# Attention's side work cut into halves: products with wo and 13 of 48 score units over two pairs of steps each, and the steps of the division set further apart

## The chip, the cores and the metric

The kernel runs on one core of a Trainium2 chip. The metric is the device time of one execution in microseconds (us). The kernel before takes 1585.26 us (median of 3 runs, 1582.82 to 1586.16).

## The reference

A transformer block on 2048 tokens of 448 features: attention with 16 heads of 28 features, then a layer that picks 8 of 4096 experts for each token and head by product keys (two lists of 64 sub-keys).

```python
h = x + A(layernorm(x))                       # A: softmax(q k^T / sqrt(28)) v for 16 heads, then @ wo
q = einsum("nd,dhc->nhc", layernorm(h), w_q)  # 16 heads, 2 x 256
s1, s2 = q[..., :256] @ k1.T, q[..., 256:] @ k2.T     # 64 sub-key scores each
t1, i1 = top8(s1); t2, i2 = top8(s2)
cand = t1[..., :, None] + t2[..., None, :]            # 64 candidates
top_s, top_e = top8(cand)                             # expert i1 * 64 + i2
g = softmax(top_s)
h2 = h + einsum("nhk,nhk,nhkd->nd", g, gelu(einsum("nd,nhkd->nhk", layernorm(h), u[top_e])), v[top_e])
```

## The kernel before

The tokens stand in four blocks of 512 (b = 0 to 3), the heads in four groups of four. A first part makes queries, keys and values. The second part, which the change is about, is attention with other work woven into it. Later parts make the matrix of expert weights G and run through all experts; they are not touched.

**Attention** is 256 steps: block b, group g, and 16 stretches of 128 keys. In a step, `scores(u + 2)` gives TensorE 12 matmuls (L593) into two S tiles, from which ScalarE makes two exponentials P (L597); then `values(u)` gives it four products of P with V, told as 8 matmuls (L675), which add up in the tile A over 16 steps. After the sixteenth, VectorE copies A to `on` (L682). S has three buffers; a step uses two. Where a step's number stands in the set `paired`, the values of this step and of the next are made together, so that two steps run as: scores, values, values, scores, and then the side work of the pair. "A pair" below means such two steps; "a free step" is one without side work.

**Side work** is made of generators. `weave` gives each a stretch of steps and calls the one whose turn comes next, so that its table (the list `work`, with `begin`) sets the order of the program on each engine. What matters here:

- `project(b)`, begun at step `begin[b]` for blocks 0, 1, 2 (block 3 comes after attention): for each of four tiles of 128 tokens, VectorE makes a high and a low half of `on` (`oh` L106, `ol` L749), TensorE multiplies them with wo (12 matmuls, L100, into the tile M), VectorE adds x and hscale (`added`, L765) and takes moments, GpSimd makes `rstd`, VectorE normalizes (`xn` L123) and splits (`hl`), and a transposing DMA writes `Xb`.
- `search(b, order)`: 16 units for each block, 48 in all. A unit is 11 matmuls of Xb with the folded key weights w (L100, into M), one eviction by ScalarE into `fresh` (L881, two buffers) and two look-ups by VectorE (`best`: 4 times MAX8 and 4 times FIND_INDEX8 each).
- `divide(n, k)`: the division by the softmax sums for each group n, spread over the 16 steps k of the next group: a DMA of the sums, `invert` (DMA in, reciprocal, DMA `rec` out), `spread` (four DMAs into `rb`, L611), `scale` (L630, VectorE).
- `pairs_of` and `places_of` (GpSimd, VectorE, and 4 transposes on TensorE for each tile, L1008), `share` (a transpose of `every`, L165), `tops`, `parts_of_up` and `parts_of_down` (GpSimd and DMA).

All side work on TensorE writes to one PSUM tile M with one buffer. `due` holds evictions that are written behind the next step's scores; `flush` writes them. The order that the generators give is kept on TensorE, VectorE, ScalarE, GpSimd and SyncE.

After the last step `divide_last`, two units of the next part (`up`, L575) and `project(3)` follow.

Of the kernel before, what the change touches and what calls it, by code (L numbers as in the profile page):

```python
# [15 lines left out]
AF = mybir.ActivationFunctionType  # L16
# [48 lines left out]
def block(ctx: ExitStack, tc: tile.TileContext, x, wqk, wv, wo, wq, k12, uT, v, cst, out):  # L65
# [32 lines left out]
    def mm_all(ps, pairs):  # L98
        for i, (l, r) in enumerate(pairs):
            nc.tensor.matmul(ps, l, r, start=i == 0, stop=i == len(pairs) - 1)  # L100
# [45 lines left out]
    class Scale:  # L146
# [21 lines left out]
        def share(self):  # L168
            self.spread()
            yield  # L170
            flush()
            pt = self.turned(P[0], "M")
            due.append(lambda: self.set(pt[:, 0]))
            yield
            flush()
# [29 lines left out]
    due = []  # L205
# [374 lines left out]
    def attention(paired):  # L580
# [51 lines left out]
        def divide(n, k):  # L632

            if k == 1:
                gather(n)
            if n % 4 == 3:
                if k == 2:
                    spread(n, sum_d[n])
                if 4 <= k < 8:
                    scale(n, slice(128 * (k - 4), 128 * (k - 3)), True)  # L640
            elif k in (3, 5, 6):
                invert(n, (3, 5, 6).index(k))
            elif k == 8:
                spread(n, rec_d[n])
            elif k == 10:
                scale(n, slice(0, 512), False)
# [83 lines left out]
    def project(b, offset=6, room=None):  # L730
# [7 lines left out]
        def tile_of(j):  # L738
# [12 lines left out]
            yield  # L751
            flush()
            pa = P[0].tile([128, 512], F32, name="M")
            mm_all(pa[:, :D], [(l[:, t], w[:, t]) for l, w in ((oh, woh), (oh, wol), (ol, woh)) for t in range(4)])
# [47 lines left out]
    PROJECT = 26  # L802
# [23 lines left out]
    def scores_of(XH, XL, w, j, turned=False):  # L826
# [6 lines left out]
        mm_all(p[:, :n], low + high if turned else high + low)  # L833
# [24 lines left out]
    def search(b, order):  # L858
# [15 lines left out]
        last = None  # L874
        g = 0
        for n, (i, j) in enumerate(order):
            if last:
                best(*last)
            turned = n + 1 == len(order) or order[n + 1][0] != i
            src = sp.tile([128, 512], F32, name="fresh", bufs=2)  # L880
            nc.scalar.activation(src, scores_of(*X[b], (loads[g, 0], loads[g, 1]), j, turned), AF.Identity, scale=gscale[:, i:i + 1])  # L881
            if turned:
                load(g + 1, 1)
                load(g + 2, 0)
                g += 1
            yield
            best(2 * i, j, src[:, :256])
            last = 2 * i + 1, j, src[:, 256:]
            yield
        best(*last)  # L890
        yield

    SEARCH = 33
# [107 lines left out]
    def to_slots(eng, b):  # L1001
        st = bg.tile([128, 2, 1024], F16, name="st", bufs=2)
        slots, gslots = st[:, 0].rearrange("p (k n) -> p k n", k=2), st[:, 1].rearrange("p (t k u) -> p t k u", k=2, u=2)
        for j in range(4):
            flush()
# [156 lines left out]
    with tc.manual_schedule(engines={ET.PE, ET.DVE, ET.Activation, ET.Pool, ET.SP}):  # L1162
        load_kv(2)
        load_kv(3)
        begin = [FOLDED + 5, 67 + 66, 69 + 128]
        a = attention({4 * h for h in range(1, H)} | {t + k for t in begin for k in (1, 7, 13, 19)}
                      | {t + 25 + 2 * n - 4 * (t > 190) for t in begin for n in range(16)})
# [26 lines left out]
        for b in range(3):  # L1194
            t = begin[b] - FOLDED
            look = search(b, [(i, j) for g in ((0, 1), (2, 3)) for i in range(4) for j in g])
            work += [(project(b), PROJECT, t, t + PROJECT), (islice(look, 1), 1, t + 16, t + 17), (store_X(b), 1, t + 36, t + 37)]
            t += 26 if b < 2 else 22
            p = 64 * b + 174 - FOLDED
            work += [(look, SEARCH, t, t + SEARCH)]  # L1200
            if b < 2:
                work += [(chain(*[pairs_of(j, nc.gpsimd) for j in range(4)]), 4 * PAIRS_POOL, t + 18, p),
                         (places_of(b, nc.scalar), PLACES, p, p + 2 * PLACES)]
            else:
                work += [(pipeline([pairs_of(j, nc.gpsimd) for j in (0, 1)], 6), 6 + PAIRS_POOL, t + 20, 257 - FOLDED)]
# [177 lines left out]
```

## Time and profile before

| | us |
|---|---|
| median of 3 runs | 1585.26 |
| the profiled execution | 1585.02 |
| its span, first to last instruction | 1583.2 |
| first exponential of attention | 156.1 |
| last pair of exponentials begins | 818.4 |
| TensorE busy in the span | 1521.8 |
| ScalarE busy in the span | 906.8 |
| VectorE busy in the span | 1171.7 |
| GpSimd busy in the span | 362.0 |

The profile is of one execution. The chain of waits follows the end back from the last instruction; in it a row has a start, a length, an engine and what ran, and "x11" is a count of matmuls. The timeline has the same with shapes, and in brackets the idle time of the engine ahead of a row with what ended it. Stretches ("windows") list each engine's busy time, then the granted clock of TensorE (1.00 is full), the share of the DMA engines and GB/s.

### The profile page before, as it was taken

How to read it: one execution, taken by the hardware profiler on the slowest of the kernel's cores; microseconds unless marked ns; L12 is line 12 of the kernel's file. 1: busy time of each engine (PE TensorE's matmuls, PEld its weight loads, DVE VectorE, ACT ScalarE, POOL GpSimd, SP SyncE). 2: the span in 40 equal slices, each digit the busy share in tenths (PEclk: the TensorE clock that was granted, in tenths of full speed). 3: DMA queues.
4: the chain of work that ended last, by engine and by line, in shares of the span. 5: the costliest groups of instructions: out<-in, count | busy, mean ns of one | idle time of the engine just before them, and what ended most of it. 6: DMA issues, size and time to landing. Idle time of an engine off the chain costs nothing.

```text
span 1583.2 us, 33148 instructions
## 1 busy us (share of the span) xinstructions
PE 1521.8 (96%) x12441; PEld 644.8 (41%) x12441; DVE 1171.7 (74%) x3947; ACT 906.8 (57%) x1220; POOL 362.0 (23%) x484
## 2 busy tenths in 40 slices
PE   5999999999999999999997999999999999999998
PEld 3444222222332233223334654455445554555444
DVE  8763365564577677667688999799998998889622
ACT  3544888898888878988873432334423343334321
POOL 1242000524245743797671000000000000000000
PEclk9999999999999999999999999999999999999999
DMA  8424787679875557578823244454344434443454
GB/s 278 142 98 127 236 272 247 204 204 288 274 227 163 192 178 229 175 209 265 292 76 113 79 144 130 129 182 118 112 133 136 152 98 151 127 139 113 122 145 133
DMA packets 176475, 270.36 MB, mean 171 GB/s; under 512 B 29949, under 2 KB 106493, under 8 KB 176313
## 3 DMA queue, kind: packets, MB, share of 16 engines
q1 hardware_dynamic: 172088, 266.14, 54.7%
q10 hardware_dynamic: 4224, 2.10, 0.5%
q8 instruction: 97, 1.59, 0.4%
q14 instruction: 66, 0.53, 0.1%
HBM read 215.91 MB, written 49.50 MB: 168 GB/s over the span
## 4 chain that ended last, share of the span: by engine, by line
PE 68%; DVE 19%; DMA 5%; POOL 3%; issue 2%; ACT 1%; SPq 1%; DVEq 0%; POOLq 0%; ACTq 0%
PE acc L1291 15%; PE M L100 12%; PE A L675 10%; PE A L100 9%; PE S L593 9%; PE pq L100 6%; DVE p L1078 3%; DVE G L1099 2%; DVE fg L1063 2%; PE M L280 2%; DMA w<-wp 1%; DVE pos L902 1%; PE A L1105 1%; DVE f L1057 1%; DVE ring L1263 1%
## 5 line engine op out<-in xcount | busy, mean ns | idle before, releaser
L597 ACT ACTIVATE P<-S,escale 128x1024 f32<-128x1024 f32 x512 | 533.4, 1123 | 74.9 <-PE S L593 69.0
L1291 PE MATMUL acc<-v,w 128*128 128x448 f16 x1536 | 308.6, 354 | 1.8 <-DVE w L1266 1.3
L675 PE MATMUL A<-P,V 128*32 128x512 f32 x2048 | 258.4, 603 | 1.9 <-DVE on L682 1.9
L593 PE MATMUL S<-qS,kS 32*128 32x512 f16 x3072 | 236.0, 379 | 3.7 <-ACT P L597 3.0
L1291 PEld LDWEIGHTS <-w 128*128 128x128 f16 x1536 | 148.0, 98 | 144.1 <-DVE w L1266 5.4
L100 PEld LDWEIGHTS <-u 128*128 128x128 f16 x1386 | 130.7, 98 | 145.0 <-issue 4.2
L100 PE MATMUL A<-Xb,u 128*128 128x512 f16 x759 | 175.2, 379 | 2.5 <-DVE G L1099 2.5
L100 PE MATMUL M<-w,Xb 128*128 128x512 f16 x704 | 166.4, 383 | 5.1 <-DVE Xb L144 3.8
L575 ACT ACTIVATE ring<-A,ugelu 128x512 f32<-128x512 f32 x69 | 47.2, 686 | 213.3 <-PE A L100 213.3
L1078 DVE TENSOR_TENSOR p<-st,iota 128x2048 f16<-128x2048 f16 x128 | 155.8, 1218 | 14.8 <-PE M L1095 8.1
L593 PEld LDWEIGHTS <-kS 32*128 32x128 f16 x3072 | 65.2, 92 | 214.1 <-issue 178.7
L1263 DVE SCALAR_TENSOR_TENSOR ring<-ring,wscale,G 128x512 f32<-128x512 f32 x128 | 92.0, 744 | 76.2 <-ACT ring L575 76.1
L100 PE MATMUL M<-Xb,u 128*128 128x512 f16 x627 | 147.5, 381 | 0.0
L100 PEld LDWEIGHTS <-Xb 128*128 128x128 f16 x704 | 64.0, 98 | 97.0 <-issue 25.2
L1265 ACT ACTIVATE w<-ring 128x512 f16<-128x512 f32 x128 | 75.9, 622 | 41.7 <-DVE ring L1263 29.1
L675 PEld LDWEIGHTS A<-P,V 128*32 128x32 f32 x2048 | 48.3, 108 | 124.3 <-issue 116.3
L900 DVE MAX8 ti<-fresh 128x8 f32<-128x64 f32 x384 | 56.8, 209 | 53.1 <-ACT fresh L881 53.0
L1135 POOL TENSOR_SCALAR raw<-raw,scale 128x512 f32<-128x512 f32 (+1 forms) x64 | 45.7, 714 | 200.5 <-DMA raw<-in_uT_dram 199.5
L575 ACT ACTIVATE ring<-M,ugelu 128x512 f32<-128x512 f32 x57 | 39.2, 687 | 89.0 <-PE M L100 87.3
L1266 DVE SCALAR_TENSOR_TENSOR w<-w,ring 128x512 f16<-128x512 f16 x128 | 84.8, 684 | 6.1 <-ACT w L1265 5.8
L1063 DVE TENSOR_TENSOR fg<-f,st 128x2048 f16<-128x2048 f16 x64 | 77.9, 1217 | 0.1
L902 DVE FIND_INDEX8 ti<-ti,fresh 128x8 uint32<-128x64 f32 x384 | 76.7, 218 | 0.0
(210 smaller groups left out, 1882.9 us busy)
## 6 DMA issues: line engine op xcount, KB each, us to landing
v<-vs SPq DMA_DIRECT2D x128, 336.0 KB
u<-us SPq DMA_DIRECT2D x126, 256.0 KB
w<-wp SPq DMA_DIRECT2D x56, 512.0 KB
kS<-ks SPq DMA_DIRECT2D x64, 256.0 KB
V<-vd SPq DMA_DIRECT2D x64, 256.0 KB
wr<-in_wq_dram SPq DMA_DIRECT2D x32, 448.0 KB
vs<-hl SPq DMA_DIRECT2D x32, 336.0 KB
seen<-in_uT_dram SPq DMA_DIRECT2D x32, 256.0 KB
```

The costliest lines, as they stand in the source:

```text
L100: nc.tensor.matmul(ps, l, r, start=i == 0, stop=i == len(pairs) - 1)
L575: gelu[0] = nc.scalar.activation(act, p, AF.Gelu_apprx_tanh, scale=ugelu).ins
L593: nc.tensor.matmul(S[j // 2][:, j % 2], kS[r, a, 128 * (k % 4):128 * (k % 4) + 128], qS[r, c], start=m == 0, stop=m == 2)
L597: nc.scalar.activation(Pt[:, 2 * i:2 * i + 2], S[i], AF.Exp, scale=escale[:, n % 4:n % 4 + 1])
L675: nc.tensor.matmul(O[n][32 * j:32 * j + 32], V[:, k % 4, j], Pt[:, j], start=k == 0, stop=k == NT - 1)
L902: nc.vector.max_index(i, t, src)
L1063: nc.vector.tensor_tensor(fg.rearrange("p t k f u -> p t k (f u)"), f1.rearrange("p t f u -> p t (f u)").unsqueeze(2).to_broadcast([128, T ...
L1078: newest[0] = nc.vector.tensor_tensor(p1, pairs(0, s, TG, 128), ids(TG, 128), op=OP.is_equal).ins
L1263: nc.vector.scalar_tensor_tensor(av, av, wscale, of_expert(b, f), op0=OP.mult, op1=OP.mult)
L1265: nc.scalar.activation(w[:, 0], a, AF.Copy, scale=1.0 / LS)
L1266: newest[0] = nc.vector.scalar_tensor_tensor(w[:, 1], w[:, 0], -LS, a, op0=OP.mult, op1=OP.add).ins
L1291: nc.tensor.matmul(acc[j][:, :D], l, r, start=f == 0 and k == 0, stop=f == 31 and k == 2)
```

## The change

Three things. First, the products with wo for blocks 0 to 2 and 13 of the 48 units of scores are cut behind their sixth matmul: the second half is written two calls later, and `paired` gives each half a pair of its own. In between the generator stands in `held`, and every other one that wants M waits in `free()`, giving up its turns. Second, the steps of `divide` are moved: spread of the inverse from k = 8 to 10, its use from 10 to 14, and a step later for each fourth group. Third, the table: `begin[1]` is 135 for 133, the search begins some 4 to 8 steps earlier within a block, between the third and fourth tile of `project`, and ends later, since 16 units take 21, 21 and 19 pairs.

```diff
@@ -95,8 +95,8 @@
     nc.gpsimd.memset(lneps, EPS)
     nc.gpsimd.memset(lnpow, -0.5)
 
-    def mm_all(ps, pairs):
-        for i, (l, r) in enumerate(pairs):
+    def mm_all(ps, pairs, lo=0, hi=None):
+        for i, (l, r) in list(enumerate(pairs))[lo:hi]:
             nc.tensor.matmul(ps, l, r, start=i == 0, stop=i == len(pairs) - 1)
 
     def copy(eng, dst, src):
@@ -168,6 +168,7 @@
         def share(self):
             self.spread()
             yield
+            yield from free()
             flush()
             pt = self.turned(P[0], "M")
             due.append(lambda: self.set(pt[:, 0]))
@@ -202,7 +203,12 @@
         for g in gens:
             yield from g
 
-    due = []
+    due, held = [], []
+
+    def free():
+
+        while held:
+            yield
 
     def flush():
 
@@ -634,15 +640,15 @@
             if k == 1:
                 gather(n)
             if n % 4 == 3:
-                if k == 2:
+                if k == 3:
                     spread(n, sum_d[n])
-                if 4 <= k < 8:
-                    scale(n, slice(128 * (k - 4), 128 * (k - 3)), True)
-            elif k in (3, 5, 6):
-                invert(n, (3, 5, 6).index(k))
-            elif k == 8:
+                if 5 <= k < 9:
+                    scale(n, slice(128 * (k - 5), 128 * (k - 4)), True)
+            elif k in (3, 6, 7):
+                invert(n, (3, 6, 7).index(k))
+            elif k == 10:
                 spread(n, rec_d[n])
-            elif k == 10:
+            elif k == 14:
                 scale(n, slice(0, 512), False)
 
         def divide_last(n):
@@ -749,9 +755,18 @@
             nc.vector.tensor_tensor(ol, of, oh, op=OP.subtract)
             yield
             yield
+            yield from free()
             flush()
             pa = P[0].tile([128, 512], F32, name="M")
-            mm_all(pa[:, :D], [(l[:, t], w[:, t]) for l, w in ((oh, woh), (oh, wol), (ol, woh)) for t in range(4)])
+            pairs = [(l[:, t], w[:, t]) for l, w in ((oh, woh), (oh, wol), (ol, woh)) for t in range(4)]
+            if not room:
+                mm_all(pa[:, :D], pairs, 0, 6)
+                held.append(b)
+                yield
+                yield
+                flush()
+                held.pop()
+            mm_all(pa[:, :D], pairs, 0 if room else 6)
             if room:
                 at = place(j, "at", "xn", 1)[:, :D]
                 nc.scalar.activation(at, pa[:, :D], AF.Identity, scale=hscale)
@@ -799,7 +814,7 @@
         nc.sync.dma_start(x_d[b][:, 4:], X[b][1])
         yield
 
-    PROJECT = 26
+    PROJECT = 30
 
     def load_X(b):
         XT = bx.tile([128, 7, 512], F16, name="Xb", bufs=2)
@@ -823,14 +838,17 @@
         return pt
 
 
-    def scores_of(XH, XL, w, j, turned=False):
+    def scores_of(XH, XL, w, j, turned=False, parts=False):
         c = slice(128 * j, 128 * j + 128)
         flush()
         p = P[0].tile([128, 512], F32, name="M")
         n = 128 * w[0].shape[1]
         pairs = products(lambda t: XH[:, t, c], lambda t: XL[:, t, c], lambda t: w[0][:, :, t], lambda t: w[1][:, :, t])
         high, low = pairs[:4] + pairs[8:], pairs[4:8]
-        mm_all(p[:, :n], low + high if turned else high + low)
+        pairs = low + high if turned else high + low
+        if parts:
+            return p[:, :n], pairs
+        mm_all(p[:, :n], pairs)
         return p[:, :n]
 
     def kept_scores(b, pools):
@@ -855,7 +873,7 @@
                 nc.scalar.activation(ring[4 * j + g], scores_of(*X[b], (w[:, 0], w[:, 1]), j), AF.Identity, scale=gscale[:, g:g + 1])
                 yield
 
-    def search(b, order):
+    def search(b, order, halved):
 
 
         loads = {}
@@ -871,26 +889,41 @@
         load(0, 1)
         load(1, 0)
         yield
-        last = None
+        waiting = []
+
+        def look():
+            if waiting:
+                best(*waiting.pop(0))
+
         g = 0
         for n, (i, j) in enumerate(order):
-            if last:
-                best(*last)
+            yield from free()
             turned = n + 1 == len(order) or order[n + 1][0] != i
+            p, pairs = scores_of(*X[b], (loads[g, 0], loads[g, 1]), j, turned, True)
+            cut = 6 if n in halved else 0
+            if cut:
+                mm_all(p, pairs, 0, cut)
+                look()
+                held.append(b)
+                yield
+                flush()
+                held.pop()
+            mm_all(p, pairs, cut)
             src = sp.tile([128, 512], F32, name="fresh", bufs=2)
-            nc.scalar.activation(src, scores_of(*X[b], (loads[g, 0], loads[g, 1]), j, turned), AF.Identity, scale=gscale[:, i:i + 1])
+            nc.scalar.activation(src, p, AF.Identity, scale=gscale[:, i:i + 1])
             if turned:
                 load(g + 1, 1)
                 load(g + 2, 0)
                 g += 1
-            yield
-            best(2 * i, j, src[:, :256])
-            last = 2 * i + 1, j, src[:, 256:]
-            yield
-        best(*last)
-        yield
-
-    SEARCH = 33
+            look()
+            if n + 1 not in halved:
+                look()
+            waiting += [(2 * i, j, src[:, :256]), (2 * i + 1, j, src[:, 256:])]
+            yield
+        look()
+        yield
+        look()
+        yield
 
     ti = {}
 
@@ -1002,6 +1035,7 @@
         st = bg.tile([128, 2, 1024], F16, name="st", bufs=2)
         slots, gslots = st[:, 0].rearrange("p (k n) -> p k n", k=2), st[:, 1].rearrange("p (t k u) -> p t k u", k=2, u=2)
         for j in range(4):
+            yield from free()
             flush()
             p = P[0].tile([128, 4, 128], F16, name="M")
             for k in range(4):
@@ -1162,9 +1196,11 @@
     with tc.manual_schedule(engines={ET.PE, ET.DVE, ET.Activation, ET.Pool, ET.SP}):
         load_kv(2)
         load_kv(3)
-        begin = [FOLDED + 5, 67 + 66, 69 + 128]
-        a = attention({4 * h for h in range(1, H)} | {t + k for t in begin for k in (1, 7, 13, 19)}
-                      | {t + 25 + 2 * n - 4 * (t > 190) for t in begin for n in range(16)})
+        begin = [FOLDED + 5, 71 + 64, 69 + 128]
+        halved = [{1, 4, 7, 10, 13}, {1, 4, 7, 10, 13}, {9, 12, 14}]
+        slots = [16 + len(h) for h in halved]
+        a = attention({4 * h for h in range(1, H)} | {t + 6 * j + k for t in begin for j in range(4) for k in (1, 3)}
+                      | {t + 17 for t in begin} | {t + 23 + 2 * n for t, m in zip(begin, slots) for n in range(m - 1)})
         weave((islice(a, FOLDED), FOLDED, 0, FOLDED), (fold[0].run(fold_p, P[0]), Fold.STEPS, 0, Fold.STEPS),
               *[(fold[0].parts(fold_p, i), Fold.PARTS, 16 * i + (18 if i < 3 else 16), 16 * i + 32 if i < 3 else FOLDED) for i in range(4)],
               (tops(US, lambda f: uT[:, f].rearrange("p t e -> p (t e)"), 512), TOPS, 1, 45), (US.share(), 3, 47, 50),
@@ -1193,16 +1229,16 @@
         work = [(a, 257 - FOLDED, 0, 257 - FOLDED), (split_wo(), 4, 1, 5)]
         for b in range(3):
             t = begin[b] - FOLDED
-            look = search(b, [(i, j) for g in ((0, 1), (2, 3)) for i in range(4) for j in g])
-            work += [(project(b), PROJECT, t, t + PROJECT), (islice(look, 1), 1, t + 16, t + 17), (store_X(b), 1, t + 36, t + 37)]
-            t += 26 if b < 2 else 22
+            look = search(b, [(i, j) for g in ((0, 1), (2, 3)) for i in range(4) for j in g], halved[b])
+            work += [(project(b), PROJECT, t, t + PROJECT), (islice(look, 1), 1, t + 10, t + 11), (store_X(b), 1, t + 36, t + 37)]
+            s = t + 23.7
+            work += [(islice(look, 1), 1, t + 18.2, t + 19.2), (look, slots[b] + 1, s, s + 2 * slots[b] + 2)]
             p = 64 * b + 174 - FOLDED
-            work += [(look, SEARCH, t, t + SEARCH)]
             if b < 2:
-                work += [(chain(*[pairs_of(j, nc.gpsimd) for j in range(4)]), 4 * PAIRS_POOL, t + 18, p),
+                work += [(chain(*[pairs_of(j, nc.gpsimd) for j in range(4)]), 4 * PAIRS_POOL, t + 44, p),
                          (places_of(b, nc.scalar), PLACES, p, p + 2 * PLACES)]
             else:
-                work += [(pipeline([pairs_of(j, nc.gpsimd) for j in (0, 1)], 6), 6 + PAIRS_POOL, t + 20, 257 - FOLDED)]
+                work += [(pipeline([pairs_of(j, nc.gpsimd) for j in (0, 1)], 6), 6 + PAIRS_POOL, t + 42, 257 - FOLDED)]
         w0 = weights(0)
 
         def first_tokens():
```

In the program that comes out, counted from its order: from step 76 on, attention had 12 pairs with a product of 12 matmuls, 48 pairs with a unit of 11, and else free steps. Now it has 24 pairs with 6 matmuls of a product, 34 with a whole unit, 13 with the first 6 and 13 with the last 5 matmuls of a unit, and 12 free steps. One unit, the last of block 2, stands behind attention's last values.

The order of ScalarE at the start of block 0's search, before; P is a step's two exponentials, x4 is two steps:

```order
L597 ACTIVATE P<-S,escale 128x1024 x204
L881 ACTIVATE fresh<-M,gscale 128x512
L597 ACTIVATE P<-S,escale 128x1024 x4
L881 ACTIVATE fresh<-M,gscale 128x512
L597 ACTIVATE P<-S,escale 128x1024 x4
```

And now:

```order
L603 ACTIVATE P<-S,escale 128x1024 x188
L913 ACTIVATE fresh<-M,gscale 128x512
L603 ACTIVATE P<-S,escale 128x1024 x16
L913 ACTIVATE fresh<-M,gscale 128x512
L603 ACTIVATE P<-S,escale 128x1024 x4
L913 ACTIVATE fresh<-M,gscale 128x512
L603 ACTIVATE P<-S,escale 128x1024 x4
L913 ACTIVATE fresh<-M,gscale 128x512
L603 ACTIVATE P<-S,escale 128x1024 x8
```

The first eviction stands 16 exponentials (8 steps) earlier, with the fourth tile of `project` behind it, and where a unit is halved, eight exponentials stand between two evictions in place of four.

The order of VectorE near the fourth tile of `project(1)`, before; `every` is what TensorE transposes next (L165), and the copy of A frees the tile for the next group's values:

```order
L630 SCALAR_TENSOR_TENSOR on<-on,onscale,rb 128x512
L123 TENSOR_SCALAR xn_30885<-xt,mv,rstd 128x448
L134 CAST hl<-xn_30885 128x384
L135 CAST hl<-xn_30885 128x64
L136 TENSOR_TENSOR hl<-xn_30885,hl 128x384
L137 TENSOR_TENSOR hl<-xn_30885,hl 128x64
L160 TENSOR_REDUCE top_216<-tops_215 128x1
L161 COPY every<-top_216 128x128
L682 COPY on<-A 128x512
```

And now:

```order
L106 CAST oh_30775<-on 128x512
L755 TENSOR_TENSOR ol_30776<-on,oh_30775 128x512
L123 TENSOR_SCALAR xn_30825<-xt,mv,rstd 128x448
L134 CAST hl<-xn_30825 128x384
L135 CAST hl<-xn_30825 128x64
L136 TENSOR_TENSOR hl<-xn_30825,hl 128x384
L137 TENSOR_TENSOR hl<-xn_30825,hl 128x64
L160 TENSOR_REDUCE top_216<-tops_215 128x1
L161 COPY every<-top_216 128x128
L780 SCALAR_TENSOR_TENSOR xt<-M,hscale,xt 128x448
```

The scaling with `rb`, which waits for a DMA, stood ahead of `every` and the copy of A, and now stands behind both (it follows the copy). The halves `oh` and `ol` of a tile stand ahead of the last tile's `xn`, where they stood behind it. At the fourth tile of `project(0)` the copy of A likewise stood behind the addition that waits for `xt`, and now stands ahead of it.

The order of VectorE behind attention's last copy of A, before; L658 to L667 are `divide_last`, and `ol` is the first of `project(3)`:

```order
L682 COPY on<-A 128x512
L658 RECIPROCAL r<-M 128x16
L660 COPY rb<-r 128x512
L667 SCALAR_TENSOR_TENSOR on<-M,onscale,on 128x128 x4
L749 TENSOR_TENSOR ol_35187<-on,oh_35186 128x512
```

And now:

```order
L688 COPY on<-A 128x512
L636 SCALAR_TENSOR_TENSOR on<-on,onscale,rb 128x512
L933 MAX ti_34372<-fresh 128x8 x4
L935 MAX_INDEX ti_34372<-ti_34372,fresh 128x8 x4
L933 MAX ti_34372<-fresh 128x8 x4
L935 MAX_INDEX ti_34372<-ti_34372,fresh 128x8 x4
L664 RECIPROCAL r<-M 128x16
L666 COPY rb<-r 128x512
L673 SCALAR_TENSOR_TENSOR on<-M,onscale,on 128x128 x4
L933 MAX ti_34476<-fresh 128x8 x4
L935 MAX_INDEX ti_34476<-ti_34476,fresh 128x8 x4
```

Four look-ups have moved behind the last copy of A: two ahead of `divide_last`, and two, of the unit that now ends the search, between `divide_last` and the first `ol`.

## The prediction

> **What bounds the kernel now.** First the page's busy times of the engines.
>
> ```profile
> span 1583.2 us, 33148 instructions
> PE 1521.8 (96%) x12441; PEld 644.8 (41%) x12441; DVE 1171.7 (74%) x3947; ACT 906.8 (57%) x1220; POOL 362.0 (23%) x484
> ```
>
> TensorE is busy nearly always, ScalarE 57% on average, but attention's 512 exponentials all fall into some 660 us, and there which of the two sets the pace has to be read step by step. The chain of waits gives free steps, a pair with a product, and pairs with a unit of scores:
>
> ```profile
> 323.05 1.01 PE S L593 x12
> ...
> 333.09 1.01 PE S L593 x12
> 334.10 1.85 PE A L675 x16
> 335.96 0.76 PE S L593 x12
> 336.71 2.38 PE M L100 x12
> ...
> 440.44 1.85 PE A L675 x16
> 442.30 0.76 PE S L593 x12
> 443.06 2.48 PE M L100 x11
> 445.54 0.76 PE S L593 x12
> 446.29 1.85 PE A L675 x16
> ```
>
> Five free steps take 333.09 - 323.05 = 10.04, so 2.01 each, and the scores show 1.01 in place of 0.76: TensorE waits for buffers. The pace is ScalarE's, by the timeline of ScalarE:
>
> ```profile
> 529.58 10.15 ACT L597 ACTIVATE P<-S,escale 128x1024 f32<-128x1024 f32 x10 [1.67 <-PE S L593]
> ```
>
> Ten exponentials in 10.15 is about 1.0 each, two to a step. A pair with a unit is the other way round: 1.85 + 0.76 + 2.48 + 0.76 = 5.85 (446.29 - 440.44), TensorE without a gap, while its four exponentials need 4.0. With a product it is 5.75. So TensorE loses some 0.3 us in each free step, which side work could use, and pays in full in each pair. The fold's pairs show that a pair is 3.37 plus its side work:
>
> ```profile
> 179.43 1.85 PE A L675 x16
> ...
> 182.04 1.65 PE M L280 x8
> ...
> 184.46 1.00 PE A L675 x8
> ```
>
> Side work of 1.65 gives 184.46 - 179.43 = 5.03, and 3.37 + 1.65 = 5.02. This holds down to ScalarE's 4.0, plus the eviction where there is one.
>
> **Splitting.** From the first pair with a product to the values of the last pair, the same chain ends as:
>
> ```profile
> 817.98 1.85 PE A L675 x16
> 819.83 0.33 PE M L1008 x4
> 820.16 1.53 PE A L675 x8
> 821.70 2.48 PE S L100 x11
> ```
>
> The stretch is 817.98 - 334.10 = 483.9. By kinds it is 12 x 5.75 + 48 x 5.85 + 59 free steps x 2.01 = 468.4; the other 15.5 are waits and transposes, below.
>
> What do half units cost? A stop after few matmuls stands in the timeline:
>
> ```profile
> 421.05 1.02 PE L100 MATMUL M<-w,Xb 128*128 128x512 f16 x4 [0.58 <-DMA w<-wp]
> ...
> 422.00 0.83 PE L593 MATMUL S<-qS,kS 32*128 32x512 f16 x12
> ```
>
> Four matmuls held TensorE from 421.05 to 422.00, 0.95; eleven hold it 2.48; so one is 0.219, and a start costs 0.08. Six cost 1.39, five 1.17; six of a product 1.23 (half of 2.38 and half of a start). Half pairs are then 4.76, 4.54 and 4.60. ScalarE has 4.0 in each, and 0.69 (the eviction, below) in one of the two of a unit: 8.7 of 9.3, so TensorE still sets the pace, closely. By the counts of the new order: 24 x 4.60 + 34 x 5.85 + 13 x 9.30 + 12 x 2.01 = 454.3. Against 468.4 that is **14.1 less**, about 0.57 for each of 25 splits. Bounds: if each of the 13 evictions pushed exponentials back by its full 0.69, 9.0 of it are gone; I take none, since the pair has 0.6 to spare. The upper end is 14.6 (the rounding of a start).
>
> **Waits that should go.** VectorE holds TensorE up in four places, by the timeline:
>
> ```profile
> 387.66 1.06 PE L675 MATMUL A<-P,V 128*32 128x512 f32 x8 [1.87 <-DVE on L682]
> 526.28 0.93 PE L100 MATMUL M<-woh,oh 128*128 128x448 f16 x4 [0.59 <-DVE oh L106]
> 555.07 0.33 PE L165 MATMUL M<-ct,every 128*128 128x128 f32 x1 [1.76 <-DVE every L161]
> 698.63 0.93 PE L100 MATMUL M<-woh,oh 128*128 128x448 f16 x4 [1.63 <-DVE oh L106]
> ```
>
> In two of them the clock fell too, by the windows (the number behind POOL's count is the granted clock):
>
> ```profile
> 388.00:390.00 2.00, 2.00 (x24) 0.42 (x20) 1.97 (x6) 0.08 (x1) 1.10 (x2) 0.75 1.07 410
> 390.00:392.00 2.00, 2.00 (x12) 0.14 (x8) 1.24 (x3) 2.00 (x2) 1.84 (x3) 0.50 1.07 375
> ...
> 556.00:558.00 2.00, 2.00 (x9) 0.72 (x6) 1.87 (x4) 1.75 (x2) 1.66 (x2) 0.56 0.86 191
> 558.00:560.00 2.00, 2.00 (x7) 0.71 (x5) 0.00 (x0) 0.37 (x1) 0.00 (x0) 0.58 0.93 306
> ```
>
> Idle 1.87 + 0.59 + 1.76 + 1.63 = 5.85; lost clock 2 x (0.25 + 0.50 + 0.44 + 0.42) = 3.2; together 9.1. The chain names what VectorE itself waited for:
>
> ```profile
> 376.40 8.42 DMA xt<-in_x_dram
> ...
> 535.55 9.54 DMA rec<-r
> ...
> 546.41 2.34 DMA rb<-rec
> ```
>
> In the first place the copy of A stood behind an addition waiting for `xt`; that addition now comes two steps (4 us) later, behind the copy. In the third, `every` stood behind the scaling that waits for `rb`; the spread now has three steps after `rec` and not two, the scaling comes four steps after the spread and not two, and `every` stands ahead of it. In the second and fourth, `oh` stood behind the former tile's `xn` (in the fourth that waited for GpSimd's rstd); now it stands ahead. What is late next: behind `every` the scaling stands ahead of the reduction that frees M; if `rb` has landed, copy and scaling cost some 1.5 us beside scores of 0.76. The w loads still wait for their buffer (0.58 above), though several now have a half pair more. I take **9.1** as gone, and the other 6.4 (transposes, w, the slow last steps) as staying. Bounds: 13.2 gone (all but seven transposes of 0.33), or none, or one more wait of the costliest kind, 1.76 + 1.7.
>
> [...]
>
> **The end of attention.** One unit has moved behind the last values, and four look-ups with it. Before, from the start of the last pair's values to the next part's first unit: 821.70 - 817.98 = 3.72. Now: the values wait for the last exponentials, whose scores stand 1.17 (the half unit) plus 0.76 ahead: ScalarE needs 0.17 + 2 x 1.0 + 0.1 from the scores' end, the first values fill 1.17 to 2.1, the second follow at 2.3 and end at 3.2, so 2.05 after their start; then the transposes 0.33, their eviction 0.8, the unit 2.48: 5.7. That is 1.9 later. Then the look-ups:
>
> ```profile
> L900 DVE MAX8 ti<-fresh 128x8 f32<-128x64 f32 x384 | 56.8, 209 | 53.1 <-ACT fresh L881 53.0
> ...
> L902 DVE FIND_INDEX8 ti<-ti,fresh 128x8 uint32<-128x64 f32 x384 | 76.7, 218 | 0.0
> ...
> L881 ACT ACTIVATE fresh<-M,gscale 128x512 f32<-128x512 f32 x48 | 33.0, 687 | 19.7 <-PE M L100 17.0 <-PE S L593 1.4 <-DVE ti L902 1.0
> ```
>
> A look-up is 4 x (56.8 + 76.7) / 384 = 1.4 with little overlap. The first two lie beside the `up` unit; the last two, 2.7, stand ahead of the first `ol`, and then VectorE sets the pace of `project(3)`. So **4.5 more**, between 1.9 (VectorE catches up) and 6.5 (2.0 more for M's evictions).
>
> **Sum.** The profiled execution took 1585.0 (span 1583.2 and 1.8 around it), 0.2 under the median. 1585.0 - 14.1 - 9.1 + 4.5 = **1566.3**. The rest, from 850 us on, is untouched, and the fold keeps its order on TensorE.
>
> **Rivals.**
> 1. *The waits come back elsewhere.* VectorE waits for the same DMAs, 8 to 10 us long, with as many instructions, and the chain of each pair is now TensorE's own. For it: w is loaded earlier, into the stretch where `xt` took 8.42. Against it: the rows above all have their cause moved. Time: 1566.3 + 9.1 = 1575.4.
> 2. *The eviction of the one M tile is exposed.* If TensorE stood for 0.69 in each of the 25 split units, 17.3 come back: 1583.6. The rows speak against it: from a unit's end (445.54) to the next M matmul lie 0.76 + 1.85 + 0.76 = 3.37. [...]
> 3. *Slower: look-ups come late for `fresh`.* They are now given out two at a time after the next eviction, and `fresh` has two buffers. An eviction that waits holds all exponentials behind it. Half a look-up, 0.7, at each of 47 units is 33, so 1599; it decides from 18.7 / 47 = 0.40 each. The row of `fresh` speaks against it: 1.0 us for VectorE in all 48.
> 4. *The change does less than it says*: `free()` gives up turns, so work slides out of attention to where nothing hides it. The order shows one unit there, counted above; two more pairs' worth would be 1566.3 + 2 x 5.85 = 1578.
>
> **How the numbers follow.** The forecast 0.60, rival 1 0.22, rival 2 0.05, rival 3 0.06, rival 4 0.07. The forecast's own bounds: 1585.0 - 14.6 - 13.2 + 1.9 = 1559.1 and, with 5.1 of the splits, no wait gone and 6.5 at the end, 1586.4. The range 1559 to 1581 takes in rivals 1 and 4 and leaves out rivals 2 and 3 and the corner where all goes badly at once. A difference of 0.2% (3.2 us) is about what a measurement of this kernel can tell from no change. Faster by more: forecast, rivals 1 and 4 nearly whole: 0.87. Within: most of rival 2: 0.05. Slower: rival 3 and a little of 1: 0.08.
>
> **What would show it.** Pairs with a half unit at 4.5 to 4.8 in the chain, whole ones at 5.85; no idle time of TensorE over 1 us between 340 and 800, and the clock at 1.00 there; the last pair of exponentials near 794 in place of 818; and the first product of `project(3)` 21 us earlier than before, its third part (with `ol`) 19. Half pairs above 5.0 would make the splitting wrong, a row of idle time ended by VectorE the second term, and ScalarE waiting for look-ups would be rival 3.

## The result and the profile after

| | before | after |
|---|---|---|
| median, first measurement (us) | 1585.2 (4 runs) | 1574.67 (4 runs, 1572.41 to 1577.35) |
| ratio to before, with its 95% interval | | 0.9936 [0.9917, 0.9956] |
| median, second measurement (us) | 1581.82 (11 runs) | 1574.83 (6 runs, 1571.21 to 1575.74) |
| ratio, with its interval | | 0.9945 [0.9930, 0.9959] |
| the profiled execution | 1585.02 | 1577.35 |

The change makes the kernel 0.6% faster, 7 to 10.5 us of medians where 18.9 were forecast (1585.2 to 1566.3): 37 to 56% of the forecast. The page of after begins with its span and the busy times:

```profile
span 1575.6 us, 33133 instructions
...
PE 1514.2 (96%) x12441; PEld 648.0 (41%) x12441; DVE 1173.9 (75%) x3947; ACT 907.2 (58%) x1220; POOL 362.8 (23%) x484
```

Line numbers have grown by 6 to 36: exponentials are L603 now, values L681, `fresh` L913, the look-ups L933 and L935, the copy of A L688, `ol` L755.

**Half pairs.** The chain of waits of after, at two pairs with half a product, and then at the two halves of a unit:

```profile
348.96 1.85 PE A L681 x16
350.81 0.76 PE S L599 x12
351.57 1.24 PE M L100 x6
352.81 0.84 PE S L599 x12
353.65 1.85 PE A L681 x16
...
408.18 1.85 PE A L681 x16
410.03 0.76 PE S L599 x12
410.79 1.40 PE M L100 x6
412.19 0.76 PE S L599 x12
412.95 1.85 PE A L681 x16
414.80 0.76 PE S L599 x12
415.56 1.19 PE M L100 x5
416.75 0.90 PE S L599 x12
417.64 1.85 PE A L681 x16
```

A half pair of a product takes 353.65 - 348.96 = 4.69, the two of a unit 412.95 - 408.18 = 4.77 and 417.64 - 412.95 = 4.69. Six and five matmuls cost 1.24, 1.40 and 1.19, as worked out; what is longer is the second scores, 0.84 and 0.90 in place of 0.76. ScalarE's timeline at the product's half pair and at the unit's second one shows why:

```profile
351.67 4.13 ACT L603 ACTIVATE P<-S,escale 128x1024 f32<-128x1024 f32 x4 [0.57 <-PE S L599]
...
415.66 2.12 ACT L603 ACTIVATE P<-S,escale 128x1024 f32<-128x1024 f32 x2 [0.49 <-PE S L599]
417.67 0.69 ACT L913 ACTIVATE fresh<-M,gscale 128x512 f32<-128x512 f32 x1
```

In both, ScalarE first stands idle until the pair's first scores are there. S has three buffers and a step uses two, so the second scores need a buffer that the pair's first exponential still reads. That exponential ends at 352.78 in the first of these pairs and at 416.77 in the second, and in both all but the first two matmuls of the second scores begin 0.05 behind it. So a pair cannot be shorter than this chain (times of the timelines): values 1.86, from the first scores to the exponential 0.92, the exponential 1.11, 0.05, and 0.75 for the scores that are left, together 4.69. Of the 36 full pairs with 1.24 or 1.19 of side work 35 take 4.69 to 4.70 (the first takes 4.74), whether an eviction stands in them or not. TensorE's own work would be 3.37 + 1.24 = 4.61 and 4.56, and ScalarE is idle for 0.57 in each product's half pair: neither engine's work sets this time, the chain through the buffers of S does. Only with 1.40 of side work is TensorE's sum, 4.77, the longer one. No run changed the number of S's buffers, so this is read from the times in the traces; in the chains of both runs of experiment 5 and of the second of 7, too, the second scores take 0.90 behind 1.19 of side work.

**Waits.** The waits at all four places where VectorE held TensorE are gone, and the windows at the two that also lost clock show 1.00 now.

```profile
388.00:390.00 2.00, 2.00 (x23) 0.44 (x16) 2.00 (x15) 1.43 (x3) 1.56 (x4) 1.00 1.08 374
...
556.00:558.00 2.00, 2.00 (x24) 0.48 (x20) 2.00 (x19) 2.00 (x3) 0.00 (x0) 1.00 0.89 238
```

New ones stand elsewhere. TensorE's timeline of after has four worth naming:

```profile
428.64 1.02 PE L100 MATMUL M<-w,Xb 128*128 128x512 f16 x4 [0.91 <-DMA w<-wp]
...
548.93 1.46 PE L100 MATMUL M<-w,Xb 128*128 128x512 f16 x6 [0.66 <-DMA qS<-qs]
...
694.35 2.53 PE L100 MATMUL M<-w,Xb 128*128 128x512 f16 x11 [1.03 <-DVE xt L780]
...
787.81 0.38 PE L1042 MATMUL M<-ident,sl 128*128 128x128 f16 x4 [1.36 <-ACT fresh L913]
```

The second stands behind the transpose of `every`, at the third of the old places. The row names a DMA, but the reduction that frees M (`top`, L179) ends only at 548.88, behind the copy of A and the scaling on VectorE (547.32 to 548.67); in the second execution, below, the same wait of 0.65 is put down to it. The prediction had named this order as what is late next. The last comes from ScalarE, which waited for look-ups twice:

```profile
787.07 0.69 ACT L913 ACTIVATE fresh<-M,gscale 128x512 f32<-128x512 f32 x1 [2.34 <-DVE ti L935]
...
794.44 0.69 ACT L913 ACTIVATE fresh<-M,gscale 128x512 f32<-128x512 f32 x1 [2.12 <-DVE ti L935]
```

This is the third rival, at 2 of 48 units. In the kernel before, ScalarE's timeline has such a wait at the first of these two places, step 249:

```profile
804.13 0.69 ACT L881 ACTIVATE fresh<-M,gscale 128x512 f32<-128x512 f32 x1 [0.99 <-DVE ti L902]
```

So the 1.0 us in the row with which the prediction spoke against this rival was not spread over 48 units: it was one wait, where VectorE was already late.

**The end.** The chain of after behind attention's last pair:

```profile
803.75 2.14 PE A L681 x16
...
806.96 2.53 PE M L100 x11
809.50 2.37 PE S L100 x11
...
815.53 1.12 DVE on L673 x4
816.65 0.50 DVE ti L933 x4
817.15 0.79 DVE ti L935 x4
817.94 0.49 DVE ti L933 x4
818.43 0.79 DVE ti L935 x4
819.22 0.59 DVE ol L755
```

From the last values to the first `up` unit it is 809.50 - 803.75 = 5.75, and two look-ups (2.57) stand ahead of `ol`.

**Where the time went.** The first exponential of a step tells where the step stands; project(3)'s last product (the last of a group of 20 matmuls) closes the part that the change touches. Two executions of each kernel are known (the second ones are experiments below):

| stretch (us) | before | before again | after | after again |
|---|---|---|---|---|
| start of the span to step 76 | 334.0 | 334.0 | 335.4 | 333.2 |
| step 76 to step 255 | 484.4 | 479.5 | 467.3 | 466.7 |
| step 255 to project(3)'s last product | 37.8 | 37.8 | 44.2 | 43.9 |
| the rest | 727.1 | 727.1 | 728.8 | 725.6 |

Attention's stretch is 12.7 to 17.1 shorter; 6.1 to 6.4 of that is given back right behind it. The first and last stretch hold the same work in all four (in the first, only steps of the division have moved); what differs there between the profiled executions of the two kernels, 1.4 and 1.7, goes with one stretch of 3.41 at half clock more in each: in after one begins at 160.38, where before has none ahead of step 76, and three against two lie behind project(3), the ones at the very end aside.

### The profile page after: what moved, and what is told of

Read it like the earlier page. It is cut to its first block, busy times and chain, and to the rows that moved or that the text cites. A ratio compares the mean times of both kernels' runs of the same rounds, so it can differ in the third digit from the quotient of the medians.

```text
span 1575.6 us, 33133 instructions
## 1 busy us (share of the span) xinstructions
PE 1514.2 (96%) x12441; PEld 648.0 (41%) x12441; DVE 1173.9 (75%) x3947; ACT 907.2 (58%) x1220; POOL 362.8 (23%) x484
## 4 chain that ended last, share of the span: by engine, by line
PE 68%; DVE 22%; DMA 4%; POOL 2%; issue 2%; ACT 1%; SPq 0%; DVEq 0%; POOLq 0%; ACTq 0%
PE acc L1327 14%; PE M L100 11%; PE A L681 11%; PE S L599 10%; PE A L100 9%; PE pq L100 6%; DVE p L1112 4%; DVE G L1133 2%; DVE fg L1097 2%; PE M L286 2%; DVE f L1091 1%; DVE ring L1299 1%; PE A L1139 1%; DVE pos L935 1%; DVE w L1302 1%
## 5 line engine op out<-in xcount | busy, mean ns | idle before, releaser
L603 ACT ACTIVATE P<-S,escale 128x1024 f32<-128x1024 f32 x512 | 536.1, 1117 | 63.3 <-PE S L599 58.4
L681 PE MATMUL A<-P,V 128*32 128x512 f32 x2048 | 253.2, 601 | 0.0
L599 PE MATMUL S<-qS,kS 32*128 32x512 f16 x3072 | 227.9, 378 | 2.8 <-ACT P L603 2.1
L100 PE MATMUL A<-Xb,u 128*128 128x512 f16 x759 | 178.4, 384 | 2.5 <-DVE G L1133 2.5
L681 PEld LDWEIGHTS A<-P,V 128*32 128x32 f32 x2048 | 50.7, 109 | 126.6 <-issue 119.8
L933 DVE MAX8 ti<-fresh 128x8 f32<-128x64 f32 x384 | 56.6, 208 | 31.0 <-ACT fresh L913 30.9
L935 DVE FIND_INDEX8 ti<-ti,fresh 128x8 uint32<-128x64 f32 x384 | 76.7, 217 | 0.0
```

The lines of the kernel that those rows point to most:

```text
L599: nc.tensor.matmul(S[j // 2][:, j % 2], kS[r, a, 128 * (k % 4):128 * (k % 4) + 128], qS[r, c], start=m == 0, stop=m == 2)
L603: nc.scalar.activation(Pt[:, 2 * i:2 * i + 2], S[i], AF.Exp, scale=escale[:, n % 4:n % 4 + 1])
L681: nc.tensor.matmul(O[n][32 * j:32 * j + 32], V[:, k % 4, j], Pt[:, j], start=k == 0, stop=k == NT - 1)
L935: nc.vector.max_index(i, t, src)
```

## The experiments

Kernels that are compared by medians ran on one chip, beside the kernel before: experiments 2 to 4 and the first of 5 beside 1582.46 us (19 runs), 1, 6 and the second of 5 beside 1581.82 (11), and 7 beside 1582.29 (11). "Step 76 to 255" and "the end" are the second and third stretch of the table.

**1. A second execution of each.** The changed kernel and the kernel before, as they are.

> The changed kernel once more, beside the next three. Theory: the late look-ups come back at the same steps (249 and 251, 2 to 2.5 and 1.2 us), since VectorE's order and work are fixed; the waits for w (steps 113 and 217) are DMA and vary by up to 2 us; attention from step 76 to 255 takes 465 to 469 us, the median 1571.5 to 1573.5 on this chip. Rival (the late look-ups are a chance of one execution): they are under 0.5 us, attention 463 to 465.

> The kernel before once more, for a second trace. Theory (the four waits for VectorE belong to the kernel, since they follow from its order): the exponentials of steps 98/99, 149, 160/161 and 213 are late again by 1.3, 0.7, 2.9 and 1.7 us within 0.4 each, and attention from step 76 to 255 takes 483 to 486 us. Rival (they hang on when a DMA lands and differ from one execution to the next, as the times of before, 1577 to 1587, may say): at least one of the four is gone or more than 1 us longer, and attention takes 478 to 482 or over 487.

After again: 1574.83; 466.7; the late look-ups came back (ScalarE idle for 2.27 and 2.11 at steps 249 and 251), the wait for w at step 113 did not. Before again: 479.5, and TensorE's timeline has the four places once more, but shorter:

```profile
387.29 1.06 PE L675 MATMUL A<-P,V 128*32 128x512 f32 x8 [1.50 <-DVE on L682]
...
523.86 0.93 PE L100 MATMUL M<-woh,oh 128*128 128x448 f16 x4 [0.58 <-DVE oh L106]
...
551.84 0.33 PE L165 MATMUL M<-ct,every 128*128 128x128 f32 x1 [0.95 <-DVE every L161]
...
693.21 0.93 PE L100 MATMUL M<-woh,oh 128*128 128x448 f16 x4 [1.12 <-DVE oh L106]
```

They add up to 4.15, and no sign of a half clock stands in attention: between 330 and 820 no row of twelve scores takes over 1.16, where one in a half-clock stretch of experiment 5 takes 1.46. So the places belong to the kernel and their size to the execution (the theory and its rival each had half of it): 9.1 in the first, 4.15 in this one.

**2. No splits.** The new table and division, with whole products and units.

```diff
-        halved = [{1, 4, 7, 10, 13}, {1, 4, 7, 10, 13}, {9, 12, 14}]
+        halved = [set(), set(), set()]
...
-            if not room:
-                mm_all(pa[:, :D], pairs, 0, 6)
-                held.append(b)
-                yield
-                yield
-                flush()
-                held.pop()
-            mm_all(pa[:, :D], pairs, 0 if room else 6)
+            mm_all(pa[:, :D], pairs)
```

(The two idle calls stand ahead of the product, and `paired` keeps only its second pair.)

> The change's table and division, but products with wo and units all whole (16 pairs to a block's search). Theory (the new order alone took the four waits away, a split is worth 0.4 to 0.45, and the end loses its extra unit): against the change 25 x 0.43 + 1.8 in attention lost, 3.6 of late look-ups and 5 to 6 behind attention gained: 1576 to 1579, that is 6 to 9 us under the kernel before, and the end of attention as long as before (765 to 768 behind the last exponentials). Rival A (splitting is what gave the gain, the waits come back where pairs are whole): 1583 to 1586. Rival B (splitting gives nothing): 1566 to 1570.

1580.19 beside 1582.46 of before, ratio 0.9985 [0.9971, 0.9999]; step 76 to 255 476.7, the end 37.6. The end was as the theory had it and the four waits are gone, but the time is only 2.3 under before, between the theory and rival A: 476.7 stands 7.7 under the first execution of before and 2.8 under the second, and late look-ups (3.03 and 1.49 of idle ScalarE at steps 249 and 251) are here too. So the order alone is worth 2 to 3 us beside the second execution of before, less than the 4.15 that its four places took, and most of the gain is the splits': against the next kernel, with 22 splits and nearly the same end, 1580.19 - 1571.93 = 8.3, 0.38 each.

**3. Block 2's units whole.**

```diff
-        halved = [{1, 4, 7, 10, 13}, {1, 4, 7, 10, 13}, {9, 12, 14}]
+        halved = [{1, 4, 7, 10, 13}, {1, 4, 7, 10, 13}, set()]
```

> The three units of block 2 that were halved are whole again, so its search takes 16 pairs and the last unit and all look-ups stand inside attention. Theory (what the change lost is the work it pushed behind attention, and the look-ups that came late for fresh): attention loses 3 x 0.4 for the splits and 1.8 for the unit that comes back, and gains the 3.6 of the two late look-ups, so exponentials from step 76 to 255 begin over about 466.7 us in place of 467.3; from the last exponentials to the end 766 to 768 us in place of 772.9; together about 1569 in place of 1574.7. Rival (project(3) is paced by VectorE and its own chain, and the unit stood beside that): the end stays at 771 to 773 and the time at 1573 to 1576.

1571.93, ratio 0.9940 [0.9923, 0.9957]; the end is 38.9 in place of 44.2, as the theory said. The chain shows what left it: the first `up` unit begins 806.57 - 802.85 = 3.72 behind the last values, as before, with no unit of scores between.

```profile
802.85 1.85 PE A L681 x16
...
806.57 2.48 PE S L100 x11
```

But step 76 to 255 took 468.9, not 466.7: of the late look-ups only 0.55 is left (step 251), and waits for w of 1.8 and 0.4 have come in. The time lies between the theory's and the rival's, and its ratio cannot be told from the change's.

**4. Three buffers of fresh.**

```diff
-            src = sp.tile([128, 512], F32, name="fresh", bufs=2)
+            src = sp.tile([128, 512], F32, name="fresh", bufs=3)
```

> The change with three buffers of fresh in place of two; every engine's order stays. Theory (the two late evictions near the end of block 2's search wait for a buffer only): the idle times of 2.34 and 2.12 of ScalarE ended by look-ups are gone, attention is 3.6 us shorter (464 from step 76 to 255), the time about 1571. Rival (VectorE is full there, so what ScalarE no longer waits for is waited for by something else, the transposes or the look-ups behind attention): attention or the end gives it back, and the time stays at 1573 to 1576.

1571.48, ratio 0.9931 [0.9914, 0.9948]; step 76 to 255 463.2, the end 43.8 as in the change. Of the evictions that waited 2.34 and 2.12 for look-ups the first has no idle time ahead of it now, and the second waits for its own unit alone:

```profile
789.39 0.69 ACT L913 ACTIVATE fresh<-M,gscale 128x512 f32<-128x512 f32 x1 [0.61 <-PE M L100]
```

The order on every engine is the same, so the 3.5 to 4.0 us that attention is shorter are the buffer's. The theory holds by the trace; the ratio's interval overlaps with the change's.

**5. The old steps of the division,** twice.

```diff
-                if k == 3:
+                if k == 2:
...
-                if 5 <= k < 9:
+                if 4 <= k < 8:
...
-            elif k in (3, 6, 7):
+            elif k in (3, 5, 6):
...
-            elif k == 10:
+            elif k == 8:
                 spread(n, rec_d[n])
-            elif k == 14:
+            elif k == 10:
```

> The change with the old steps of the division; the halves of products and units stay. In VectorE's order the scaling with rb of block 1's last tile then stands ahead of every again, two steps behind its spread. Theory (the moved steps took away the wait at every, the halves' order took away the other three): one idle time of TensorE of 1 to 2 us ended by every comes back near the fourth tile of project(1), with up to 1.7 of halved clock: 1576.5 to 1578.5. Rival (with halves the chain leaves VectorE room, and the division's steps change nothing): no such row, 1574.7 within 1.

> The change with the old steps of the division, once more, beside the change itself, since its median lay some 4 us over that of the change's other variants while its traced execution showed no wait for rb. Theory (rb lands late in some executions, and then the scaling holds every and the halves of on): median 3 to 4 us above the change's, and if the traced execution is a usual one, a wait of 1 to 3 us at the fourth tile of a block, ended by VectorE. Rival (the halves gave VectorE enough room, the difference was chance and halved clock): median within 1.5 us of the change's, attention within 1 of its time.

1576.23 (ratio 0.9963 [0.9949, 0.9977]), and beside the change 1575.42 against 1574.83 (to the kernel before 0.9952 [0.9938, 0.9965], the change 0.9945): no difference that can be told. Yet the traces differ, alike in both runs, and neither theory had it so. No wait for `every` comes back, although the scaling ahead of it stood 3.58 us for rb: in the second run `every` is begun at 544.90 and transposed at 550.53, so the table leaves room enough. A wait for w comes instead, 2.42 and 2.27 us near step 113. VectorE's, SyncE's and TensorE's timelines of the second run, each a row or two:

```profile
417.48 0.75 DVE L636 SCALAR_TENSOR_TENSOR on<-on,onscale,rb 128x512 f32<-128x512 f32 x1 [6.56 <-DMA rb<-rec]
```

```profile
421.88 0.34 SPq L1155 DMA_DIRECT2D seen<-in_v_dram  x1
422.26 0.43 SPq L813 DMA_DIRECT2D xd<-Xb  x1
422.73 0.43 SPq L814 DMA_DIRECT2D xd<-Xb  x1
423.60 2.00 SPq L886 DMA_DIRECT2D w<-wp  x2
```

```profile
426.47 1.68 PE L100 MATMUL M<-w,Xb 128*128 128x512 f16 x7
430.42 1.80 PE L100 MATMUL M<-w,Xb 128*128 128x512 f16 x4 [2.27 <-DMA w<-wp]
```

The scaling holds VectorE for 6.56; behind it stand the reductions that free `seen`, so on SyncE the loads of `seen`, the stores of Xb and the load of w all come late, and w is issued 4.6 us ahead of its use (423.60 to 428.15) and needs 6.8. In the change the same load is issued 6.5 ahead (421.26) and takes 7.34. Against this loss, the old steps give back 0.7 at step 161, 1.5 at step 249 and 1.3 to 1.6 in the end: the two come to nothing.

**6. A second buffer for the low half of w,** with block 2 whole.

```diff
-                loads[n, k] = w = sp.tile([128, 4, 4, 128], F16, name="w", tag="w" + "hl"[k], bufs=2 - k)
+                loads[n, k] = w = sp.tile([128, 4, 4, 128], F16, name="w", tag="w" + "hl"[k], bufs=2)
```

> Block 2's units whole (as in the first experiment) and two buffers for the low half of w in place of one. Theory (the loads of w wait for their buffer, which the last unit of a head gives free only shortly before the next one needs it): the idle times of TensorE ended by w at steps 113, 217 and 241 (0.1, 1.5 and 2.0 in the run with block 2 whole) are gone, attention takes 465 to 466 us in place of 468.9, the end is as there, the median 3 to 4 us under that run's. Rival (the loads are late by their own length or queue, not for the buffer): the waits stay between 1 and 4 us in all, the median within 1 of that run's.

1570.60, ratio 0.9919 [0.9904, 0.9935], 4.2 under the change on the same chip: the fastest kernel of the study. Its intervals overlap with the change's own, so the trace has to say what it is worth: step 76 to 255 468.4, only 0.5 under experiment 3. The wait at step 241 shrank from 1.8 to 0.3; the one at step 217 stayed (1.40: it is not for w, but for the addition that frees M, the row `xt` above); and late look-ups came back, 1.5 of idle ScalarE at each of steps 249 and 251. That they came because TensorE now arrives earlier at a VectorE that is full is likely, but not shown. The rival is closer: where one wait went, the next stood behind it.

**7. The parts put together:** experiment 6 with the old division, and the same with three buffers of fresh in place of the second of w.

> Block 2's units whole, two buffers for the low half of w, and the old steps of the division: the parts of the change that paid, without those that the runs so far showed to cost something. Theory: the old division gives back what it gave in its own two runs (0.66 at step 161, up to 1.5 at step 249, 1.4 between the last exponentials and project(3)'s last product), and the second buffer takes away the wait for w at step 113 that came with it (2.6 and 3.9 there): attention 466 to 467.7 in place of 468.4, the end 37.5 in place of 39.0, the median 1.5 to 3 us under the run with both buffers (ratio 0.990 to 0.9915 to the kernel before). Rival (w is late with the old division whatever its buffers, because its loads stand behind other transfers): a wait over 2 us at step 113 again, attention 469 to 472, ratio 0.992 to 0.994.

> The same, with three buffers of fresh in place of the second one of w. Theory: no late look-up anywhere, but w late again: over 2 us at step 113 and about 2 at step 241, attention 468 to 471, ratio 0.9915 to 0.9935, slower than its neighbour by 1.5 to 3 us. Rival (the look-ups set more than w): attention under 467 and the median under its neighbour's.

1572.68, 0.9929 [0.9902, 0.9955], and 1572.54, 0.9926 [0.9906, 0.9946]; step 76 to 255 472.0 and 470.5. Neither beats experiment 6. In both w is late again (2.30 and 2.55 of idle TensorE near step 113). The second buffer does not help, since the load is not waiting for one: its chain in the first of the two reads

```profile
416.64 0.75 DVE on L636
...
421.04 0.33 SPq L1155
...
421.43 0.42 SPq L813
...
422.37 8.70 DMA w<-wp
```

This is the rival of the first expectation: the load stands behind other transfers on SyncE. It is issued 6.4 ahead of its use, although its buffer is free; with the same buffers and the moved steps (experiment 6) it is issued about 2.5 earlier, counted from step 76. And its own 8.70 is longer than 6.4. So the moved steps of the division do have a use, and it is this load, not the wait for `every` that the prediction gave them.

## Why the prediction was right, and which terms were off

- *Direction, and the place of the gain*: right. Half pairs fell to 4.69 to 4.77 (4.5 to 4.8 foretold), whole ones stayed at 5.85, the four waits left, attention became shorter.
- *Splitting, -14.1*: mis-sized. The rule that a pair is 3.37 plus its side work "holds down to ScalarE's 4.0, plus the eviction where there is one" was the step that failed, and with it "so TensorE still sets the pace, closely". It compared the work of each engine and left out the chain that runs through both: scores, the exponential that reads them, and the next scores in its buffer. That chain is 4.69, so a half pair does not fall below it. Product halves measure 4.69 for 4.60, unit halves 4.77 + 4.69 = 9.46 for 9.30. A split product gains 5.75 + 4.02 - 2 x 4.69 = 0.39 (by the exponentials' starts in both kernels 9.87 - 9.42 = 0.45), a split unit 5.85 + 4.02 - 9.46 = 0.41, where 0.57 was taken: 10 for 25 splits, and 0.38 each by experiment 2. That lies within the bounds given (5.1 to 14.6), but these were set for another cause, evictions that push exponentials back.
- *Waits that go, -9.1*: right for the execution it was read from, since all four left and the lost clock with them (0.66 stands in the third place now); not for the kernel. The second execution of before has 4.15 there. The terms were summed from one profiled execution, in which the clock happened to halve twice within attention (0.50 in 390 to 392, 0.56 in 556 to 558). The moved division steps were named as part of the cause for one of the four; experiment 5 shows that the table and the halves do it without them.
- *Waits taken to stay as they were*: wrong by the third rival. It was priced at 33 us everywhere or nothing; it came at 2 units near the end of block 2's search, where `pairs_of`, casts and look-ups fill VectorE, for 3.5 to 4.0 us (experiment 4). The row that spoke against it was an average over 48 units; where in time its 1.0 us lay would have shown the place.
- *The end, +4.5*: right in its place, in part by luck in its size. The first part is 5.75 where 5.7 was worked out. From the last values to project(3)'s last product it is 846.82 - 803.75 = 43.07 in after and 856.14 - 817.98 = 38.16 before: 4.9 more, up to 1.7 of it, half of 3.41, a second stretch of half clock, which the prediction had not counted (after has them from 822.56 and 832.80, before one from 839.56). Experiment 3 took nearly all of it away. The signs named for it (project(3) 21 and 19 us earlier) came at 12.8 and 11.1, because the two terms above fell short and attention began later.
- *The rest, untouched*: it is, but the profiled execution of after is 1.4 longer ahead of step 76 and 1.7 longer behind project(3), and has in each a stretch of half clock more than that of before.

For the two profiled executions the ledger is: forecast -18.7, measured 1577.35 - 1585.02 = -7.7; of the 11.0 between, splits 3.5 to 4, late look-ups 3.5 to 4, half clock outside attention 3.1, the end 0.4. It was the sum of several small misses to one side that made 18.7 into 7.7. The median of 1574.67 lies beside rival 1's 1575.4, but by chance: rival 1 gave all of the 9.1 back and let the splits stand. Of it came true the waits for w, for M and behind `xt` (0.91, 0.66 and 1.03), which are no more than what the forecast let stay. A rest of under 1 us may lie in the waits for DMAs, which differ from one execution to the next (0.91 for w at step 113 in after, none there in after again).

## What to carry to other kernels

Cutting a unit of work in two so that both halves fit where an engine has slack pays only down to the longest chain that runs from engine to engine through the buffers: add up that chain (here scores, exponential, next scores in its buffer: 4.69) and not only the work of each engine, and expect less than the busy times promise (0.4 of 0.57 here). An idle time in a row over many instructions says little until one has looked where in time it lies. A wait that ends with a DMA should be measured in two executions before its removal is priced, and one that is removed is priced together with the next wait behind it (here the late look-ups, w, and the addition that frees M). Work that is pushed past the end of a stage comes back at full price (here the end took 44.2 in place of 37.8); to leave three units whole was as good as to split them.

## What the runs showed of the hardware

In both profiled executions the granted clock of TensorE stands at 0.50 for 3.41 us at a time: in before from 389.00, 556.26, 839.56, 1071.67 and 1331.08 on, in after from 160.38, 822.56, 832.80, 907.90, 1122.94 and 1324.32 (one at the very end of each span aside). Within a trace these starts lie whole multiples of 3.4133 apart, to 0.01 (556.26 - 389.00 = 49 x 3.4133). In the 3.41 ahead of them TensorE was idle for 1.87, 1.76, 2.66, 2.02 and 2.20 in before and for 1.61, 2.48, 2.12, 1.47, 1.99 and 2.21 in after, so twice for less than half of that time (1.61 and 1.47). In other stretches of that length, a whole multiple of it away from the starts, it was idle about as long and the clock of the next 3.41 stayed at 1.00: 1.63 (696.20 to 699.62) and 1.99 (1129.70 to 1133.11) in before, 1.50 (815.74 to 819.15) and 1.54 (1416.48 to 1419.90) in after. In these two traces the idle time alone does not tell which wait is followed by half clock. A wait of experiment 5 shows the same: the one for w was 2.42 in one run and 2.27 in the other, and these are the windows behind them, first of the run with 2.42:

```profile
430.00:432.00 2.00, 2.00 (x24) 0.62 (x26) 0.00 (x0) 1.09 (x2) 0.00 (x0) 1.00 1.04 394
```

and of the run with 2.27:

```profile
430.00:432.00 2.00, 1.58 (x4) 0.40 (x3) 0.16 (x1) 0.00 (x0) 0.00 (x0) 0.63 1.03 400
```

Behind the longer wait the clock stayed at 1.00 up to 436; behind the shorter one it was 0.63 and then 0.52 (432 to 434). By the timelines it is 434.05 - 429.72 = 4.33 from the end of the longer wait to the next unit's first matmul into M, and 436.33 - 430.42 = 5.91 from the end of the shorter one, with the same matmuls between. What decides it is not shown.
